# Second MLP: the first products of the last three tiles put ahead of the output products of tiles 13 to 17, with a third lnT buffer and a second l16 buffer

## The chip, the core and the metric

The kernel runs on one core of a Trainium2 chip. The metric is the device time of one execution in microseconds (us); less is better. The core has a matrix engine (TensorE, PE in the profile, its weight loads PEld), three engines for elementwise work (VectorE = DVE, ScalarE = ACT, GpSimd = POOL), and SyncE (SP), whose queue here issues all DMAs. Each engine works through its own instructions in the order in which they were written; semaphores tie the engines together.

## The reference

Three stages follow each other: a linear attention, a first MLP with a leaky ReLU, and a second MLP with a softmax-gated activation, a layer norm and an output product. The change is in the second MLP alone:

```python
def _moe2_ref(x, w_in, w_out, g_ln):          # x 2304 x 512, w_in 512 x 1024, w_out 1024 x 512
    h = x @ w_in                              # "first product"
    e = np.exp(h - np.max(h, axis=-1, keepdims=True))
    sm = e / (np.sum(e, axis=-1, keepdims=True) + 1e-09)
    solu = h * sm
    mu = np.mean(solu, axis=-1, keepdims=True)
    var = np.mean((solu - mu) ** 2, axis=-1, keepdims=True)
    ln = (solu - mu) / np.sqrt(var + 1e-06) * g_ln
    return (ln @ w_out).astype(np.float32)    # "output product"
```

## The kernel before

The 2304 tokens are 18 tiles of 128 tokens, numbered 0 to 17 here. Each float32 operand of a large product is held as two fp16 parts (a value cut to fp16 and the remainder), and a product is three groups of fp16 matmuls: high by high, high by low, low by high.

**The stages of one tile in the second MLP.** In the text, inN is the first product of tile N, outN its output product, lnTN and l16N its buffers.

- **inN** (`mlp2_in`, line L1177): 24 matmuls of 128x512 on PE, three groups of 8, into a PSUM buffer h2 (h in the rows, as the profile leaves buffer numbers out). There are two h2 buffers.
- **The middle** (`mlp2_mid`), mostly on DVE: the row maximum mx (L1203), nb (L1205), on ACT the exponential e with its sum (L1208), then three small steps (L1212 to L1214) and so = h*e*r (L1215), which is the last reader of the h2 buffer. Then the two halves of the statistics (L1220), their aggregate (L1221), ve (L1222), on POOL the power rs (L1223), rs scaled (L1227), the normalised ln (L1228, shown as e because it takes a buffer of that pool), on POOL its fp16 part l16 (L1233), on DVE the remainder (L1235). Two small steps of the following tile, u (L1192, L1194), stand among these.
- **The transposes** (L1240): two DMA transposes issued by SP bring the two halves of l16 into a buffer lnT.
- **outN** (`mlp2_out`, line L1253): 24 matmuls of 128x512 which read lnT as weights, into a PSUM buffer h1 (also two).
- **The store** (`store`): ACT copies h1 with a scale into osb (L1262), one buffer, and SP issues the DMA to the output (L1268, or two DMAs at L1271 for a tile that is split over two sequences, as tile 17 is).

**What sets the order.** The program's order is made when the kernel is built, by the class `Issue`: an event simulation in which every stage is a generator with a priority (a lower number goes first), buffers are counted as room, and each engine takes the ready piece of work with the lowest priority number. A product is queued in pieces of 8 matmuls. What comes out is a fixed list of instructions for each engine; on the chip, an engine whose next instruction has to wait stands still, even if a later one could run. The second MLP's outputs have priority 1002, its first products 1003 up to a tile number z, and those from z on 1001. So a first product with 1003 is put into the list only where no output product is ready, and one with 1001 goes ahead of every output product as soon as an h2 buffer is free.

```python
    BUFS = dict(raw=2, scr=2, hl=2, T=2, ke=4, qe=2, qf=2, qT=2, x=2, x16=2, kv16=2, a=2, h1=2, y=2, xT=2,
                lk=2, g32=2, wraw=3, sg=1, v=2, kv=1, y16=1, h2=2, o=1, e2=2, so=1, l16=1, lnT=2, osb=1, v16=1, kf=2)
    BUFS.update(X["bufs"])
    ...
            if z < NTILE:                                    # at the end of mlp2_in(a, z)
                yield "go", mlp2_in(z, NTILE), 1001
    ...
        sch.go(mlp2_out(), 1002)
        sch.go(mlp2_in(0, NTILE - X["tail"]), 1003)
```

Before, `tail` is 1: only in17 has the priority 1001. There are two lnT buffers and one l16 buffer.

Of the kernel before, what the change touches and what calls it, by code (L numbers as in the profile page):

```python
# [21 lines left out]

X = {'NF': 1, 'EQ': [0, 1], 'bufs': {'qe': 2, 'v': 2, 'qf': 1, 'ke': 2, 'hl': 1, 'x': 4, 'g': 6, 'sg': 3, 'qT': 4, 'x16': 2, 'scr': 3, 'T': 2, 'kf': 2, 'v16': 1, 'wraw': 3, 'raw': 2, 'y16': 1}, 't0': 418.54, 'tb': 82.11, 'w1': 131.17, 'w1s': 10.01, 'w2': 172.22, 'w2s': 4.94, 'b0': -3.87, 'b1': 157.98, 'dk': 3.59, 'dq': 11.23, 'dl': 4.75, 'c1': 81.02, 'c2': 330.62, 'pw2': 700.82, 'wlo': [0, 2, 8, 10, 12, 13, 23, 24, 25, 26, 29, 31, 33, 35, 37, 38, 40, 41, 42, 44, 45, 46], 'vd': 431.89, 'warm': 10, 'psq': ['k11', 'k14', 'k15', 'k2', 'k3', 'k5', 'k7', 'q0', 'q1', 'q12', 'q15', 'q5', 'q8', 'q9'], 'ya': [1, 2, 3, 9, 12, 13, 14, 16, 17, 18, 20, 21, 22, 23, 25, 26, 28], 'EK': [0, 1, 2, 3, 4, 5, 8], 'pkv': 528.48, 'tail': 1, 'sg': [0, 8, 9, 10, 11, 14, 15, 17, 18, 19, 21, 22, 26, 27, 28, 29, 30, 31], 'off': {'w13': -14.7, 'w5': -30.7, 'w14': 26.4, 'k1': -250.2, 'q1': -363.9, 'w2': 350.0, 'w15': -88.3, 'w4': 32.0, 'w10': -33.7, 'w23': 200.4, 'w18': 88.3, 'w24': 240.3, 'w28': -174.0, 'q17': 307.2, 'w1': -201.9, 'q10': 28.7, 'k8': 106.6, 'w21': -43.9, 'k2': 79.3, 'k15': -121.9, 'k3': -134.3, 'w20': -29.3, 'w26': 230.4, 'w6': 31.1, 'q5': 23.9, 'k6': -67.8, 'w7': -53.2, 'q3': -0.6, 'w16': -93.6, 'w25': -25.5, 'w12': 100.4, 'w9': 46.6, 'w19': -77.9, 'w0': 3.9, 'k16': -35.8, 'w17': -13.4, 'k13': 66.1, 'q15': -91.7, 'w31': 51.4, 'k14': 90.6, 'q6': 57.8, 'q7': -18.0, 'w22': 30.7, 'w8': 14.0, 'k11': -16.2, 'q14': -55.4, 'v1': 138.2, 'e2': 31.5, 'w29': 42.1, 'e1': -2.7, 'k5': -29.3, 'q13': -19.5, 'q16': -120.7, 'q11': -76.4, 'e3': 84.3, 'w3': 4.5, 'w30': 16.0, 'v0': -191.6, 'k0': -35.0, 'v3': -23.5, 'k17': 33.4, 'k9': -8.2, 'q12': 2.6, 'k10': 46.2, 'k4': 9.0, 'w27': -9.0, 'q2': 3.1, 'q0': 4.3, 'q9': -1.0, 'v2': -1.6}, 'pe': -759.15, 'KH': [2, 3], 'vb': 544.54}


class Issue:
# [126 lines left out]
def linear_attention_moe_kernel(  # L155
# [29 lines left out]
    KW = 72  # L185
    NG0, NG = NP, X["bufs"].get("g", 7)
    NX = 3
    NF = X["NF"]
    EQ = X["EQ"]
    off = X["off"].get  # L190

# [49 lines left out]

    BUFS.update(X["bufs"])
    sch = Issue(dict(BUFS, g0=NG0, g=NG, v16=0))
# [54 lines left out]
    def cut(x, s, h, l, e="V2"):  # L298

        yield "op", "A", 0.61, lambda: A.activation(out=h, in_=x, func=AF.Copy, scale=s)  # L300
        yield "op", e, 0.67, lambda: V.scalar_tensor_tensor(
            out=l, in0=x, scalar=s, in1=h, op0=ALU.mult, op1=ALU.subtract)

    def cut_weight(n, x, s, h, l):

        if n not in X["wlo"]:
            yield from cut(x, s, h, l)
# [1050 lines left out]
```

## Time and profile before

| what | value |
|---|---|
| time, median of 3 runs | 735.59 us (735.02 to 735.67) |
| the profiled execution's own time | 737.42 us |
| its span (first to last instruction of the profile) | 735.6 us |
| PE busy in the span | 697.9 us, 95% |
| DVE busy | 517.4 us, 70% |
| ACT busy | 385.4 us, 52% |
| POOL busy | 163.3 us, 22% |
| granted PE clock, mean | 0.963 |

The first row is what counts. The profile shows one execution: its span, the busy time of each engine, and for each idle stretch of an engine what ended it. The granted clock is the share of PE's full clock that was allowed: 1.00 is its upper level of 2.4 GHz, 0.50 its lower level of 1.2 GHz; a value between is a mean over both.

### The profile page before, as it was taken

What the parts mean: (1) busy time and instruction counts of PE and PEld (TensorE: products, weight loads), DVE (VectorE), ACT (ScalarE), POOL (GpSimd) and SP (SyncE); (2) the same over time, 40 slices, a digit from 0 to 9 for tenths busy, and PEclk for the clock granted to TensorE, in tenths of its full rate; (3) what the DMA queues carried; (4) which work ended last, traced back from release to release, by engine and by line L of the source; (5) the groups of instructions that cost most, each with busy time, mean ns of one, the idle gap of its engine ahead of it and who ended that gap; (6) DMA issues with size and microseconds to landing.
All of it is one profiled execution on the core that took longest, in us unless ns stands there. A gap on an engine that the chain in (4) does not pass through costs nothing.

```text
span 735.6 us, 13252 instructions
## 1 busy us (share of the span) xinstructions
PE 697.9 (95%) x4888; PEld 451.9 (61%) x4888; DVE 517.4 (70%) x1351; ACT 385.4 (52%) x854; POOL 163.3 (22%) x205
## 2 busy tenths in 40 slices
PE   5967899999999999999999999999999999999977
PEld 3957788656775775767757667566654444444432
DVE  5889898899888656977756428974078577577571
ACT  5797699767787754677725425655132121221120
POOL 3233344522621101112101002353001102011110
PEclk7965899999999999999999999999999999999997
DMA  9588976449757441574315434711024324314232
GB/s 272 165 252 217 229 228 172 93 105 155 143 74 153 105 102 44 103 140 75 59 29 86 73 94 161 211 38 30 1 44 86 94 50 87 85 44 108 65 81 62
DMA packets 183984, 81.21 MB, mean 110 GB/s; under 512 B 146800, under 2 KB 175472, under 8 KB 183920
## 3 DMA queue, kind: packets, MB, share of 16 engines
q1 hardware_dynamic: 183920, 80.38, 47.8%
q8 instruction: 38, 0.62, 0.3%
q14 instruction: 26, 0.21, 0.1%
HBM read 41.75 MB, written 4.72 MB: 63 GB/s over the span
## 4 chain that ended last, share of the span: by engine, by line
PE 80%; DMA 6%; DVE 6%; ACT 3%; issue 2%; SPq 1%; POOL 0%; ACTq 0%; DVEq 0%; POOLq 0%
PE y L1063 20%; PE h L1018 18%; PE h L1253 13%; PE h L1177 13%; PE h L1012 3%; PE y L1059 3%; PE kv L788 2%; DMA T<-hl 2%; DMA qT<-qf 2%; PE a L708 1%; PE a L927 1%; PE a L709 1%; PE kv L783 1%; DMA raw<-in_k_dram 1%; PE a L705 1%
## 5 line engine op out<-in xcount | busy, mean ns | idle before, releaser
L1063 PE MATMUL y<-w,g 128*128 128x512 f16 x768 | 175.4, 379 | 0.3 <-DVE g L1036 0.3
L1018 PEld LDWEIGHTS <-w 128*128 128x128 f16 x1536 | 148.2, 98 | 24.9 <-issue 1.6
L1063 PEld LDWEIGHTS <-g 128*128 128x128 f16 x768 | 73.5, 98 | 78.9 <-DVE g L1036 0.8
L1018 PE MATMUL h<-xy,w 128*128 128x256 f16 x960 | 110.9, 273 | 0.5 <-DVE g L1036 0.4
L1253 PE MATMUL h<-wo,lnT 128*128 128x512 f16 x432 | 98.8, 387 | 4.7 <-DMA lnT<-l 4.7
L1253 PEld LDWEIGHTS <-lnT 128*128 128x128 f16 x432 | 42.9, 100 | 57.9 <-DMA lnT<-l 5.2
L1177 PE MATMUL h<-wi,xy 128*128 128x512 f16 x336 | 75.5, 379 | 0.0
L1034 ACT ACTIVATE h<-h 128x512 f32<-128x512 f32 x64 | 38.1, 595 | 68.5 <-PE h L1018 68.1
L1036 DVE TENSOR_TENSOR g<-h,g 128x512 f16<-128x512 f32 x64 | 43.9, 686 | 37.3 <-ACT g L1035 37.1
L1018 PE MATMUL h<-xT,w 128*128 128x256 f16 x576 | 67.8, 272 | 0.2
L1208 ACT ACTIVATE e<-h,nb,u 128x1024 f32<-128x1024 f32 x18 | 21.7, 1203 | 67.7 <-DVE nb L1205 56.6
L727 ACT ACTIVATE qe<-a,nb,sc 128x128 f32<-128x128 f32 x128 | 47.6, 466 | 17.5 <-DVE nb L718 10.6
L1177 PEld LDWEIGHTS <-xy 128*128 128x128 f16 x336 | 32.9, 98 | 38.8
L715 DVE TENSOR_REDUCE mx<-a 128x4 f32<-128x512 f32 x63 | 42.8, 684 | 16.4 <-PE a L709 12.7
L1262 ACT ACTIVATE osb<-h,c_out 128x512 f32<-128x512 f32 x18 | 12.4, 687 | 78.3 <-PE h L1253 42.0
L894 POOL TENSOR_SCALAR qf<-qe 128x512 f16<-128x512 f32 x32 | 21.6, 675 | 127.2 <-DMA qT<-qf 58.6
L1223 POOL TENSOR_TENSOR rs<-ve,mhalf 128x1 f32<-128x1 f32 x18 | 9.9, 549 | 156.1 <-DVE ve L1222 146.3
L1035 ACT ACTIVATE g<-h 128x512 f16<-128x512 f32 x64 | 38.4, 601 | 1.2
L727 ACT ACTIVATE ke<-a,nb,sc 128x128 f32<-128x128 f32 x88 | 33.0, 487 | 10.4 <-DVE nb L718 9.3
L1203 DVE TENSOR_REDUCE mx<-h 128x1 f32<-128x1024 f32 x18 | 21.9, 1219 | 16.1 <-PE h L1177 16.1
L708 PE MATMUL a<-omA,T 128*128 128x128 f16 x216 | 30.7, 226 | 2.1 <-DMA T<-hl 1.9
L897 DVE SCALAR_TENSOR_TENSOR qf<-qe,qf 128x512 f16<-128x512 f32 x32 | 25.3, 791 | 10.0 <-POOL qf L894 9.9
(190 smaller groups left out, 1215.1 us busy)
## 6 DMA issues: line engine op xcount, KB each, us to landing
wraw<-in_moe_w_in_dram SPq DMA_DIRECT2D x24, 512.0 KB, 5.6
wraw<-in_moe_w_out_dram SPq DMA_DIRECT2D x24, 512.0 KB, 3.3
v<-in_v_dram SPq DMA_DIRECT2D x12, 512.0 KB, 5.2
raw<-in_k_dram SPq DMA_DIRECT2D x8, 512.0 KB, 4.4
raw<-in_q_dram SPq DMA_DIRECT2D x8, 512.0 KB, 4.3
out_dram<-osb SPq DMA_DIRECT2D x16, 256.0 KB, 2.3
v<-in_v_dram SPq DMA_DIRECT2D x6, 128.0 KB, 3.8
lnT<-l SPq DMA_TRANSPOSE x36, 3.2
```

The lines of the kernel that those rows point to most:

```text
L708: PE.matmul(ps[:, h, :], lhsT=st["T"][:, 2 * h + hh, :], rhs=omA, start=True, stop=False)
L715: yield "op", "V", 0.6, lambda: V.tensor_reduce(out=mx, in_=w["ps"], axis=AX.X, op=ALU.max)
L727: A.activation(out=t[:, h, :], in_=w["ps"][:, h, :], func=AF.Exp, scale=st["sc"], bias=w["nb"][:, h:h + 1])
L897: yield "op", "V2", 0.6, lambda: V.scalar_tensor_tensor(out=w["f"][:, :, 1, :], in0=w["e"], scalar=2.0 ** 14, in1=w["f"][:, :, 0, :], op0= ...
L1012: PE.matmul(ps[:, f, :], lhsT=stash(w1, c * KC + kc)[:, o:o + 128], rhs=xT[j][:, kc, :], start=(kc == 0), stop=(kc == KC - 1))
L1018: PE.matmul(ps[:, f, :], lhsT=w1[:, c * KC + kc, w, o:o + 128], rhs=xT[j][:, :, xo + kc, :], start=(n == 0), stop=(n == 3 * KC - 1))
L1034: yield "op", "A", 0.48, lambda: A.activation(out=ps, in_=ps, func=AF.Prelu, scale=2.0 ** -19, alpha=0.01)
L1035: yield "op", "A", 0.48, lambda: A.activation(out=gg[:, 0], in_=ps, func=AF.Copy)
L1036: yield "op", "V", 0.6, lambda: V.tensor_tensor(out=gg[:, 1], in0=ps, in1=gg[:, 0], op=ALU.subtract)
L1063: PE.matmul(y_ps[j][t], lhsT=gg[:, a, f, ts], rhs=w2[:, 2 * p + f, w, :], start=(ends[0] and f == 0 and n == 0), stop=(ends[1] and f == 1 ...
L1177: PE.matmul(ps[:, f, :], lhsT=yT[i][:, a + c, :], rhs=W["i"][:, 2 * c + f, w, :], start=(j == 0 and c == 0), stop=(j == 2 and c == KC - 1))
L1253: PE.matmul(ps, lhsT=t[:, a, f, :], rhs=W["o"][:, f, w, :], start=(j == 0 and f == 0), stop=(j == 2 and f == KF2 - 1))
```

## The change

Three numbers in the table `X` change: `tail` from 1 to 3, so that in15, in16 and in17 have the priority 1001, and two new entries in `bufs`: three lnT buffers in place of two, two l16 buffers in place of one. Both lie in one pool of SBUF. The core of the diff (the line is the whole table; the rest of it is the same):

```diff
-X = {'NF': 1, ... 'raw': 2, 'y16': 1}, 't0': 418.54, ... 'tail': 1, ...
+X = {'NF': 1, ... 'raw': 2, 'y16': 1, 'lnT': 3, 'l16': 2}, 't0': 418.54, ... 'tail': 3, ...
```

Since the order comes out of the build, the built programs tell what moves. In the lists below h2, xy and xT are a first product's target and input, h1 and lnT those of an output product; the numbers behind a name tell one allocation from another.

**PE, the end of its list.** Only the first matmul of each run of equal ones is shown (their weight loads are left out); a run is 24 matmuls, or part of them where the same target comes again. Before, from the last third of in14 (h2_8545) on: out12 (h1_8631), in15 (h2_8643) with out13 (h1_8706) inside, in16 (h2_8753) with out14 (h1_8773) inside, in17 (h2_8845), out15, out16, out17:

```order
L1177 MATMUL h2_8545<-wi_6395,xy7_1975 128x512
...
L1253 MATMUL h1_8631<-wo_6396,lnT_8591 128x512
...
L1177 MATMUL h2_8643<-wi_6395,xy7_1975 128x512
...
L1253 MATMUL h1_8706<-wo_6396,lnT_8664 128x512
...
L1177 MATMUL h2_8753<-wi_6395,xT_6073 128x512
...
L1253 MATMUL h1_8773<-wo_6396,lnT_8731 128x512
...
L1177 MATMUL h2_8845<-wi_6395,xT_6073 128x512
...
L1253 MATMUL h1_8886<-wo_6396,lnT_8856 128x512
...
L1253 MATMUL h1_8953<-wo_6396,lnT_8942 128x512
...
L1253 MATMUL h1_8983<-wo_6396,lnT_8964 128x512
```

With the change, from the same place: out12 (h1_8626) in three pieces of 8 matmuls, with in15 (h2_8651), in16 (h2_8702) and in17 (h2_8767) whole between and behind them, then out13 to out17 in a row:

```order
L1177 MATMUL h2_8545<-wi_6395,xy7_1975 128x512
...
L1253 MATMUL h1_8626<-wo_6396,lnT_8578 128x512
...
L1177 MATMUL h2_8651<-wi_6395,xy7_1975 128x512
...
L1177 MATMUL h2_8702<-wi_6395,xT_6073 128x512
...
L1177 MATMUL h2_8767<-wi_6395,xT_6073 128x512
...
L1253 MATMUL h1_8788<-wo_6396,lnT_8664 128x512
...
L1253 MATMUL h1_8878<-wo_6396,lnT_8757 128x512
...
L1253 MATMUL h1_8920<-wo_6396,lnT_8844 128x512
...
L1253 MATMUL h1_8955<-wo_6396,lnT_8903 128x512
...
L1253 MATMUL h1_8983<-wo_6396,lnT_8944 128x512
```

out13 and out14 have moved behind in17; the number of matmuls is the same. Ahead of this place PE's list is unchanged.

**SP, the end of its queue.** The transposes of a tile (two, of one shape) and the stores of results. Before, from the transposes of tile 12 on:

```order
L1240 DMA_TRANSPOSE lnT_8591<-l16_8577 128x8x128 x2
L1268 DMA out_0_dram<-osb_8628 128x512
L1240 DMA_TRANSPOSE lnT_8664<-l16_8633 128x8x128 x2
L1268 DMA out_0_dram<-osb_8692 128x512
L1240 DMA_TRANSPOSE lnT_8731<-l16_8720 128x8x128 x2
L1268 DMA out_0_dram<-osb_8750 128x512
L1268 DMA out_0_dram<-osb_8820 128x512
L1240 DMA_TRANSPOSE lnT_8856<-l16_8826 128x8x128 x2
L1268 DMA out_0_dram<-osb_8937 128x512
L1240 DMA_TRANSPOSE lnT_8942<-l16_8930 128x8x128 x2
L1240 DMA_TRANSPOSE lnT_8964<-l16_8952 128x8x128 x2
L1268 DMA out_0_dram<-osb_8984 128x512
```

With the change, from the same place (the last store, of tile 17, follows in both):

```order
L1240 DMA_TRANSPOSE lnT_8578<-l16_8564 128x8x128 x2
L1268 DMA out_0_dram<-osb_8627 128x512
L1240 DMA_TRANSPOSE lnT_8664<-l16_8633 128x8x128 x2
L1240 DMA_TRANSPOSE lnT_8757<-l16_8740 128x8x128 x2
L1268 DMA out_0_dram<-osb_8789 128x512
L1240 DMA_TRANSPOSE lnT_8844<-l16_8811 128x8x128 x2
L1268 DMA out_0_dram<-osb_8879 128x512
L1240 DMA_TRANSPOSE lnT_8903<-l16_8874 128x8x128 x2
L1268 DMA out_0_dram<-osb_8921 128x512
L1240 DMA_TRANSPOSE lnT_8944<-l16_8933 128x8x128 x2
L1268 DMA out_0_dram<-osb_8956 128x512
L1268 DMA out_0_dram<-osb_8984 128x512
```

The transposes of tile 14 now stand ahead of the store of tile 12, those of tile 15 between the stores of tiles 12 and 13, those of tile 16 between the stores of 13 and 14 (before, behind the store of 15), those of tile 17 between the stores of 14 and 15.

**DVE, one of three like places** (tiles 3, 8 and 13; here tile 3). A piece of the difference, with its + and -:

```order
 L1203 TENSOR_REDUCE mx2_7675<-h2_7583 128x1
 L1192 TENSOR_SCALAR u_7683<-ikv_tok_94,ix_tok_95,c_h2_97 128x1
+L1235 TENSOR_TENSOR l16_7693<-e2_7671,l16_7693 128x1024
 L1205 TENSOR_SCALAR nb2_7676<-mx2_7675,u_7592 128x1
 L1194 TENSOR_SCALAR u_7683<-u_7683,iy_tok_96 128x1
-L1235 TENSOR_TENSOR l16_7706<-e2_7671,l16_7706 128x1024
 L1212 TENSOR_SCALAR sm_7677<-sm_7677 128x1
```

The remainder of the tile before (L1235) has moved from behind nb, on which this tile's exponential waits, to ahead of it. At the end of DVE's list the middles of tiles 15, 16 and 17 follow each other in the interleaved order that tiles 16 and 17 have before: the maximum of one tile between the statistics of the tile before, the remainder of the tile before behind so.

## Rows read from the trace of the kernel before

**Rows 1.** The page, parts 1 and 2: PE's busy time; granted clock by fortieths.

```profile
PE 697.9 (95%) x4888; PEld 451.9 (61%) x4888; DVE 517.4 (70%) x1351; ACT 385.4 (52%) x854; POOL 163.3 (22%) x205
PEclk7965899999999999999999999999999999999997
```

**Rows 2.** Stretches: length; busy PE, PEld, DVE, ACT, POOL; granted clock; DMA share; GB/s.

```profile
535.00:676.25 141.25, 141.25 (x662) 64.58 (x661) 100.46 (x217) 30.08 (x48) 22.30 (x28) 1.00 0.35 73
712.50:717.20 4.70, 0.02 (x2) 0.01 (x1) 3.96 (x7) 0.69 (x1) 1.17 (x2) 0.87 0.63 145
717.20:723.00 5.80, 5.80 (x15) 2.10 (x16) 2.18 (x3) 0.00 (x0) 1.04 (x1) 0.52 0.48 93
723.00:730.50 7.50, 7.47 (x35) 3.20 (x33) 0.00 (x0) 0.69 (x1) 0.00 (x0) 1.00 0.15 47
```

**Rows 3.** Waits from 535 us to the end: total, times, longest.

```profile
PE h L1253 <- DMA lnT<-l: 4.7, 1, 4.7
POOL l L1233 <- DMA lnT<-l: 4.2, 3, 1.4
```

**Rows 4.** The chain that ended last, from 660 us: start, length, what.

```profile
676.25 5.18 PE h L1253 x24
...
713.82 3.33 DMA lnT<-l
...
717.19 13.29 PE h L1253 x48
```

**Rows 5.** Timeline: the middle of tile 14, and the last products. (Start, length, engine, line.)

```profile
676.29 1.23 DVE L1203 TENSOR_REDUCE mx<-h 128x1 f32<-128x1024 f32 x1 [1.67 <-PE h L1177]
...
680.85 1.28 DVE L1215 SCALAR_TENSOR_TENSOR so<-h,r,e 128x1024 f32<-128x1024 f32 x1
...
681.52 0.69 ACT L1262 ACTIVATE osb<-h,c_out 128x512 f32<-128x512 f32 x1 [1.34 <-issue]
...
682.17 1.29 DVE L1220 BATCH_NORM_STATS2 bn<-so 128x6 f32<-128x512 f32 x2
...
713.31 0.34 SPq L1268 DMA_DIRECT2D out_dram<-osb  x1
...
714.81 1.28 DVE L1220 BATCH_NORM_STATS2 bn<-so 128x6 f32<-128x512 f32 x2
...
718.53 1.04 POOL L1233 TENSOR_SCALAR l<-e 128x1024 f16<-128x1024 f32 x1 [1.38 <-DMA lnT<-l]
719.61 1.23 DVE L1235 TENSOR_TENSOR l<-e,l 128x1024 f16<-128x1024 f32 x1 [1.41 <-POOL l L1233]
```

**Rows 6.** Timeline of two interleaved middles, tiles 11 and 12.

```profile
655.61 0.70 DVE L1220 BATCH_NORM_STATS2 bn<-so 128x6 f32<-128x512 f32 x1
656.23 1.21 DVE L1203 TENSOR_REDUCE mx<-h 128x1 f32<-128x1024 f32 x1
657.35 0.68 DVE L1220 BATCH_NORM_STATS2 bn<-so 128x6 f32<-128x512 f32 x1
657.95 0.20 DVE L1205 TENSOR_SCALAR nb<-mx,u 128x1 f32<-128x1 f32 x1
...
660.29 1.04 POOL L1233 TENSOR_SCALAR l<-e 128x1024 f16<-128x1024 f32 x1 [1.19 <-DVE sm L1212]
...
660.69 1.28 DVE L1215 SCALAR_TENSOR_TENSOR so<-h,r,e 128x1024 f32<-128x1024 f32 x1
...
661.89 1.22 DVE L1235 TENSOR_TENSOR l<-e,l 128x1024 f16<-128x1024 f32 x1
...
663.02 1.28 DVE L1220 BATCH_NORM_STATS2 bn<-so 128x6 f32<-128x512 f32 x2
```

**Rows 7.** Timeline: so of tile 13.

```profile
669.92 1.28 DVE L1215 SCALAR_TENSOR_TENSOR so<-h,r,e 128x1024 f32<-128x1024 f32 x1
```

**Rows 8.** The tile lnT over the span: its transposes, and their landing after issue.

```profile
L1240 SPq DMA_TRANSPOSE lnT<-l x36: 1232/1278/2082, 543.9 to 720.9; - x36
...
DMA to landing us min/median/max: 3.0/3.2/4.3
```

More of the change, by code (lines that the diff above doesn't have):

```diff
@@ L16 @@
 PSUM = bass.MemoryType.PSUM
-X = {'NF': 1, 'EQ': [0, 1], 'bufs': {'qe': 2, 'v': 2, 'qf': 1, 'ke': 2, 'hl': 1, 'x': 4, 'g': 6, 'sg': 3, 'qT': 4, 'x16': 2, 'scr': 3, 'T': 2, 'kf': 2, 'v16': 1, 'wraw': 3, 'raw': 2, 'y16': 1}, 't0': 418.54, 'tb': 82.11, 'w1': 131.17, 'w1s': 10.01, 'w2': 172.22, 'w2s': 4.94, 'b0': -3.87, 'b1': 157.98, 'dk': 3.59, 'dq': 11.23, 'dl': 4.75, 'c1': 81.02, 'c2': 330.62, 'pw2': 700.82, 'wlo': [0, 2, 8, 10, 12, 13, 23, 24, 25, 26, 29, 31, 33, 35, 37, 38, 40, 41, 42, 44, 45, 46], 'vd': 431.89, 'warm': 10, 'psq': ['k11', 'k14', 'k15', 'k2', 'k3', 'k5', 'k7', 'q0', 'q1', 'q12', 'q15', 'q5', 'q8', 'q9'], 'ya': [1, 2, 3, 9, 12, 13, 14, 16, 17, 18, 20, 21, 22, 23, 25, 26, 28], 'EK': [0, 1, 2, 3, 4, 5, 8], 'pkv': 528.48, 'tail': 1, 'sg': [0, 8, 9, 10, 11, 14, 15, 17, 18, 19, 21, 22, 26, 27, 28, 29, 30, 31], 'off': {'w13': -14.7, 'w5': -30.7, 'w14': 26.4, 'k1': -250.2, 'q1': -363.9, 'w2': 350.0, 'w15': -88.3, 'w4': 32.0, 'w10': -33.7, 'w23': 200.4, 'w18': 88.3, 'w24': 240.3, 'w28': -174.0, 'q17': 307.2, 'w1': -201.9, 'q10': 28.7, 'k8': 106.6, 'w21': -43.9, 'k2': 79.3, 'k15': -121.9, 'k3': -134.3, 'w20': -29.3, 'w26': 230.4, 'w6': 31.1, 'q5': 23.9, 'k6': -67.8, 'w7': -53.2, 'q3': -0.6, 'w16': -93.6, 'w25': -25.5, 'w12': 100.4, 'w9': 46.6, 'w19': -77.9, 'w0': 3.9, 'k16': -35.8, 'w17': -13.4, 'k13': 66.1, 'q15': -91.7, 'w31': 51.4, 'k14': 90.6, 'q6': 57.8, 'q7': -18.0, 'w22': 30.7, 'w8': 14.0, 'k11': -16.2, 'q14': -55.4, 'v1': 138.2, 'e2': 31.5, 'w29': 42.1, 'e1': -2.7, 'k5': -29.3, 'q13': -19.5, 'q16': -120.7, 'q11': -76.4, 'e3': 84.3, 'w3': 4.5, 'w30': 16.0, 'v0': -191.6, 'k0': -35.0, 'v3': -23.5, 'k17': 33.4, 'k9': -8.2, 'q12': 2.6, 'k10': 46.2, 'k4': 9.0, 'w27': -9.0, 'q2': 3.1, 'q0': 4.3, 'q9': -1.0, 'v2': -1.6}, 'pe': -759.15, 'KH': [2, 3], 'vb': 544.54}
@@ new lines @@
+X = {'NF': 1, 'EQ': [0, 1], 'bufs': {'qe': 2, 'v': 2, 'qf': 1, 'ke': 2, 'hl': 1, 'x': 4, 'g': 6, 'sg': 3, 'qT': 4, 'x16': 2, 'scr': 3, 'T': 2, 'kf': 2, 'v16': 1, 'wraw': 3, 'raw': 2, 'y16': 1, 'lnT': 3, 'l16': 2}, 't0': 418.54, 'tb': 82.11, 'w1': 131.17, 'w1s': 10.01, 'w2': 172.22, 'w2s': 4.94, 'b0': -3.87, 'b1': 157.98, 'dk': 3.59, 'dq': 11.23, 'dl': 4.75, 'c1': 81.02, 'c2': 330.62, 'pw2': 700.82, 'wlo': [0, 2, 8, 10, 12, 13, 23, 24, 25, 26, 29, 31, 33, 35, 37, 38, 40, 41, 42, 44, 45, 46], 'vd': 431.89, 'warm': 10, 'psq': ['k11', 'k14', 'k15', 'k2', 'k3', 'k5', 'k7', 'q0', 'q1', 'q12', 'q15', 'q5', 'q8', 'q9'], 'ya': [1, 2, 3, 9, 12, 13, 14, 16, 17, 18, 20, 21, 22, 23, 25, 26, 28], 'EK': [0, 1, 2, 3, 4, 5, 8], 'pkv': 528.48, 'tail': 3, 'sg': [0, 8, 9, 10, 11, 14, 15, 17, 18, 19, 21, 22, 26, 27, 28, 29, 30, 31], 'off': {'w13': -14.7, 'w5': -30.7, 'w14': 26.4, 'k1': -250.2, 'q1': -363.9, 'w2': 350.0, 'w15': -88.3, 'w4': 32.0, 'w10': -33.7, 'w23': 200.4, 'w18': 88.3, 'w24': 240.3, 'w28': -174.0, 'q17': 307.2, 'w1': -201.9, 'q10': 28.7, 'k8': 106.6, 'w21': -43.9, 'k2': 79.3, 'k15': -121.9, 'k3': -134.3, 'w20': -29.3, 'w26': 230.4, 'w6': 31.1, 'q5': 23.9, 'k6': -67.8, 'w7': -53.2, 'q3': -0.6, 'w16': -93.6, 'w25': -25.5, 'w12': 100.4, 'w9': 46.6, 'w19': -77.9, 'w0': 3.9, 'k16': -35.8, 'w17': -13.4, 'k13': 66.1, 'q15': -91.7, 'w31': 51.4, 'k14': 90.6, 'q6': 57.8, 'q7': -18.0, 'w22': 30.7, 'w8': 14.0, 'k11': -16.2, 'q14': -55.4, 'v1': 138.2, 'e2': 31.5, 'w29': 42.1, 'e1': -2.7, 'k5': -29.3, 'q13': -19.5, 'q16': -120.7, 'q11': -76.4, 'e3': 84.3, 'w3': 4.5, 'w30': 16.0, 'v0': -191.6, 'k0': -35.0, 'v3': -23.5, 'k17': 33.4, 'k9': -8.2, 'q12': 2.6, 'k10': 46.2, 'k4': 9.0, 'w27': -9.0, 'q2': 3.1, 'q0': 4.3, 'q9': -1.0, 'v2': -1.6}, 'pe': -759.15, 'KH': [2, 3], 'vb': 544.54}
```

## The prediction, as put on record before the changed kernel ran

> **What bounds the kernel now.** I began with the page. PE is busy for 697.9 of 735.6 us, and its granted clock is at 9 tenths or more in every fortieth but the first few and the last [rows 1]. So the kernel ends when PE is through its list, and what can be gained lies at the two ends of the span. The change touches the second MLP, so I cut its time into stretches. From 535 to 676.25 us PE is busy for 141.25 of 141.25 us at a clock of 1.00; from 712.50 to 717.20 it does nothing; from 717.20 to 723.00 it works at a clock of 0.52, and from 723.00 to its end at 1.00 again [rows 2]. The waits name the one that ends last: from 535 us on PE waits once, for 4.7 us, for the DMA that fills lnT; POOL waits three times for a free l16, 4.2 us in all, while PE stands still for none of these three [rows 3]. The chain of work shows the same: out12 from 676.25, at the end the transpose of tile 16 landing (3.33 us from 713.82), then out16 and out17, 13.29 us for 48 matmuls [rows 4].
>
> The price of one matmul comes from the chain: 5.18 us for the 24 of out12, 0.2158 each [rows 4]. From 676.25 PE still has out12 to out17 and in15 to in17, nine products or 216 matmuls, 46.62 us of work. It ends at 717.19 + 13.29 = 730.48, after 54.23 us [rows 4]. So **7.61 us** are lost there: 4.7 idle [rows 3], and 2.9 because the 48 matmuls at the end take 13.29 us in place of 48 x 0.2158 = 10.36 [rows 4], the half clock of [rows 2].
>
> Why it waits: tile 16's chain through DVE, POOL and the transposes is the last but one, and behind in17 PE has only out15 to do, 5.18 us. The first transpose of tile 16 was issued at 713.82, behind the store of tile 15 in SP's queue (713.31) [rows 4, 5].
>
> **The change, step by step.** No instruction is added or taken away, so the work stays at 46.62 us from 676.25. The question is whether each product finds its input. I lay PE's new list out without waits and hold every chain against it. A third of a product is 1.73 us. out12 first third 676.25 to 677.98; in15 to 683.16; second third to 684.89; in16 to 690.07; last third to 691.80; in17 to 696.98; out13 to 702.16; out14 to 707.34; out15 to 712.52; out16 to 717.70; out17 to 722.88.
>
> *The h2 buffers.* in16 takes the one of tile 14, which is free when so of tile 14 is done: 680.85 + 1.28 = 682.13 [rows 5], 2.8 us before in16 starts at 684.89. in17 takes that of tile 15. Its middle starts with the maximum: in15 ends at 683.16, the statistics of tile 14 keep DVE until 683.46 [rows 5], so it starts there. In the interleaved middles so starts 4.46 us behind the maximum (656.23 to 660.69) [rows 6]; here the second statistics half does not lie between (0.60, from 657.35 to 657.95 [rows 6]), which leaves 3.86. So of tile 15: 687.3 to 688.6, 3.2 us ahead of in17 at 691.80.
>
> *The chain of tile 16.* From so to the remainder is 1.20 and to the statistics 2.33 (660.69, 661.89, 663.02), and 0.62 later the next maximum starts (655.61, 656.23) [rows 6]. So the maximum of tile 16 starts at 687.3 + 2.95 = 690.25 (in16 ends at 690.07), its so at 694.7, the maximum of tile 17 at 697.7, so of tile 17 at 702.1, and the remainder of tile 16 at 703.3 to 704.5. ACT's copy of out12 stands in its list ahead of tile 16's exponential and can hold that up by its 0.69 [rows 5]; I leave it out, since the margins below are larger. SP has the store of tile 13 ahead of tile 16's transposes: out13 ends at 702.16, ACT starts 0.09 later (out12 ended at 676.25 + 5.18 = 681.43, its copy began at 681.52) and takes 0.69, the store's issue 0.34 [rows 4, 5], so 703.3. The first transpose is issued then, the second 1.28 later at 704.6, and each lands 3.2 us after its issue, 4.3 at the most [rows 8]: 707.8 (708.9) against out16's start at 712.52. **Margin 4.7 us.**
>
> *The chain of tile 17.* Statistics at 704.5; from there to l16 on POOL takes 3.7 (714.81 to 718.53) and to the remainder 4.8 (719.61), 1.23 long [rows 5]: 709.3 to 710.5. SP's store of tile 14 is out by 708.5. The transposes are issued at 709.3 and 710.6 and land at 713.8 (714.9), against 717.70. **Margin 3.9 us.** lnT13 and lnT14, whose buffers tiles 16 and 17 take over, are free at 702.16 and 707.34, both ahead of the issues.
>
> *The buffers.* That out13 to out17 can wait in a row needs room for several finished tiles: tile 15's transposes take lnT12 (free at 691.80), while lnT13 and lnT14 stay full. The second l16 buffer takes POOL's three waits of 4.2 us away [rows 3]; PE waits for none of them, so I set it at 0. Bounds: below 0 lies nothing but a little margin, above 0 nothing that PE could give back ahead of 712.50, where it has no idle time [rows 2].
>
> *The remainder moved ahead of nb* (three places) delays that tile's exponential by at most its 1.22 us [rows 6]. The last is tile 13, whose so ended at 669.92 + 1.28 = 671.20 [rows 7]; in15 takes its h2 buffer at 677.98. With 5.6 us to spare I set it at 0; without that cover it would be 1.22 for each place, 3.7 in all.
>
> *Behind PE.* From the last matmul to the end of the span 735.6 - 730.48 = 5.12 us pass for copy and stores [rows 4]; the same instructions stand there after.
>
> **The sum.** Both losses go: 735.6 - 7.61 = 728.0 for the span. The profiled execution's own time, 737.42, is 1.8 above its span, and the median of the runs shown, 735.59, lies at the span, so I carry the difference over to the median: 735.59 - 7.61 = **728.0 us**, 1.0% less.
>
> On the half clock: the granted clock was 1.00 up to 712.50, the engine then stood still for 4.7 us, and the clock read 0.52 in the stretch behind and 1.00 after that [rows 2]. In the second MLP it is low only behind this pause, so I let the 2.9 us go with the pause. If the clock fell for some other reason at that place, they stay, and the time is 735.59 - 4.7 = 730.9. The Trainium skill, "TensorE: Matmul & The Clock Gate", part 1, says that an engine that pauses falls to half rate and gets the full rate back by sustained work; this trace agrees. By that rule, too, the time is 728.0, not 730.9.
>
> **The rivals.** *Part of the wait stays (B).* In the tail three middles lie close together, one per 6.91 us of PE (in plus a third), while an interleaved one takes 7.4 of DVE (655.61 to 663.02 [rows 6]). If DVE or POOL hold each other up more than in the rows, out16 or out17 waits again. POOL's l16 keeps its 1.04 us beside a busy DVE and alike when DVE waits for it [rows 5, 6], which speaks against it. If 2 us more were lost for each of three middles, 6 in all, the margin of 3.9 would be overrun by 2.1: 728.0 + 2.1 = 730.1, and with the half clock again 733.0.
> The Trainium skill, "SBUF — State Buffer", section "SBUF: two separate sides", says that DVE and GpSimd share a port pair as an exclusive lock, so that the second comer waits out the whole instruction of the first. No pair of rows above shows such a wait; by that rule a busier DVE would lead to rival B.
>
> *Nothing comes of it (C).* The wait moves to another place of like size, for example in front of in16 (margin 2.8), with the half clock behind it: about 735.6. Its margin speaks against it. PE's list shows that the products do move, so that the change does nothing is excluded.
>
> *Slower (D).* PE works strictly in order, so with in17 ahead of out13 to out17 a late so of tile 15 stops five products whose inputs are ready; before, they would have run. A wait w there costs w, and if it is about as long as the present one, 2.9 more for the clock. The kernel is as before at w = 4.7 and slower by 0.2% (1.5 us) at w = 6.2, that is, if so of tile 15 ended at 698.0 in place of 688.6. At w = 8 the time is 738.9. The middles of before speak against it: from the maximum to the end of so is 5.7 us in the rows [rows 6], and D needs 14.5.
>
> **How the numbers follow.** 728.0 with both losses gone: 0.76. B: 0.13. C: 0.04. D: 0.04. The rest, 0.03, is a larger gain than I can name. A measurement of this kernel can tell about 0.2%, 1.5 us, from no change. Faster takes the forecast, nearly all of B and the rest, 0.91; same 0.04; slower 0.05, D and the worst of B. The range reaches up to 731.0, which takes in the sum with the half clock left (730.9) and the milder half of B, and down to 727.0, for the 0.2 to 0.3 us that each chain reading is uncertain by, on several of them.
>
> **What would show it.** Right: PE without an idle stretch from 535 us to its last matmul, granted clock 1.00 to the end, the last matmul near 722.9, the transposes of tiles 16 and 17 landed some 4 us before out16 and out17 begin, no wait of PE for lnT. The steps are wrong if PE waits in front of in16 or in17 (then so was late), if out16 or out17 waits (B), or if the clock reads below 1.00 in the last 20 us without a pause before it.

## The result and the profile after

The changed kernel takes 728.73 us (median of 4 runs, 727.12 to 729.64) against 735.39 us of the kernel before on the same chip; the ratio is 0.9907, with a 95% interval of 0.9887 to 0.9928. That is 6.8 us less (5.3 to 8.3). 728.0 had been forecast.

The stretches of the changed kernel, in the columns of [rows 2]; the second runs from the start of out12 to behind the last matmul:

```profile
535.00:676.25 141.25, 141.25 (x663) 64.64 (x661) 100.50 (x217) 30.10 (x48) 21.58 (x28) 1.00 0.34 73
676.25:723.00 46.75, 46.67 (x217) 20.93 (x214) 28.79 (x59) 8.51 (x13) 7.15 (x9) 1.00 0.38 90
```

PE is busy all the way at a granted clock of 1.00: the idle stretch of 4.70 us and the one at 0.52 of [rows 2] have no counterpart. The chain that ended last, in its last pieces, goes through PE alone:

```profile
676.30 1.73 PE h L1253 x8
678.03 5.18 PE h L1177 x24
683.21 1.73 PE h L1253 x8
684.94 5.18 PE h L1177 x24
690.12 1.73 PE h L1253 x8
691.85 5.18 PE h L1177 x24
697.02 25.91 PE h L1253 x120
```

These are out12 in thirds with in15, in16 and in17, then out13 to out17 as one run of 120 matmuls to 722.93; in [rows 4] the chain leaves PE for a transpose. The page's group of output products shows it too (busy, mean ns of one, idle before):

```profile
L1253 PE MATMUL h<-wo,lnT 128*128 128x512 f16 x432 | 95.9, 379 | 0.0
```

For comparisons I use one length, the **tail**: from the first matmul of out12 to the end of the last matmul, by PE's timeline. Before it is 54.37 us (676.09 to 730.46), by these first and last rows:

```profile
676.09 5.34 PE L1253 MATMUL h<-wo,lnT 128*128 128x512 f16 x24
...
717.19 13.27 PE L1253 MATMUL h<-wo,lnT 128*128 128x512 f16 x48 [4.68 <-DMA lnT<-l]
```

After, it is 46.78 us (676.14 to 722.92), 7.59 less:

```profile
676.14 1.89 PE L1253 MATMUL h<-wo,lnT 128*128 128x512 f16 x8
...
696.86 26.06 PE L1253 MATMUL h<-wo,lnT 128*128 128x512 f16 x120
```

In these rows the last matmul of a run counts with its own 0.379 us, one that another follows at once with 0.2158. So a pause costs 0.16 us more than the idle time that the row shows, and 24 matmuls at full pace read 5.34, 48 read 10.52. The 7.59 us are 4.68 + 0.16 for the pause and 2.75 (13.27 - 10.52) for the slow stretch behind it.

### The profile page after: what moved, and what is told of

Same layout as the page of the kernel before. It is cut to its first block, busy times and chain, and to the rows that moved or that the text cites. A ratio compares the mean times of both kernels' runs of the same rounds, so it can differ in the third digit from the quotient of the medians.

```text
span 727.8 us, 13253 instructions
## 1 busy us (share of the span) xinstructions
PE 693.6 (95%) x4888; PEld 450.7 (62%) x4888; DVE 513.2 (71%) x1351; ACT 386.0 (53%) x854; POOL 164.4 (23%) x205
## 4 chain that ended last, share of the span: by engine, by line
PE 80%; DMA 7%; DVE 6%; ACT 3%; issue 2%; SPq 1%; POOL 0%; DVEq 0%; ACTq 0%
PE y L1063 20%; PE h L1018 16%; PE h L1253 13%; PE h L1177 13%; PE h L1012 4%; PE y L1059 3%; PE kv L788 2%; PE a L708 2%; DMA T<-hl 2%; PE a L709 2%; PE a L927 2%; DMA wraw<-in_moe_w_in_dram 1%; DMA qT<-qf 1%; PE kv L783 1%; PE a L705 1%
## 5 line engine op out<-in xcount | busy, mean ns | idle before, releaser
L1253 PE MATMUL h<-wo,lnT 128*128 128x512 f16 x432 | 95.9, 379 | 0.0
L1012 PE MATMUL h<-xT,w 128*128 128x256 f32 x128 | 31.5, 399 | 0.8 <-DVE ar L326 0.8
```

The costliest lines, as they stand in the source:

```text
L1012: PE.matmul(ps[:, f, :], lhsT=stash(w1, c * KC + kc)[:, o:o + 128], rhs=xT[j][:, kc, :], start=(kc == 0), stop=(kc == KC - 1))
L1253: PE.matmul(ps, lhsT=t[:, a, f, :], rhs=W["o"][:, f, w, :], start=(j == 0 and f == 0), stop=(j == 2 and f == KF2 - 1))
```

## The experiments

The theory: PE's own order is the whole gain. PE waited because too little of its work stood between in16 or in17 and the products that need their results; the pause costs its length and, behind it, a stretch at half clock. The rivals: the buffers are what pays; the half clock has another cause; three tiles ahead are not needed, or more are better.

**1. The buffers alone.** The changed kernel with its buffers, but

```diff
-'tail': 3
+'tail': 1
```

> The changed kernel's three lnT and two l16 buffers, with tail left at 1. Theory (the order alone removes PE's wait): the end is as before, PE idle for about 4.7 us ahead of out16 and out16 at the half clock; time 735 to 736, within 0.2% of before. Rival (the buffers are what pays, since POOL waited 4.2 us for l16 and tiles 15 to 17 need room for finished results): the transposes of tile 16 come earlier and at least 3 us are gained, 732 or less.

Measured: 734.81 us, ratio 0.9993 (0.9979 to 1.0007), the same. The waits from 535 us on have PE's pause still in, and POOL's wait for l16 (4.2 us in [rows 3]) is gone:

```profile
PE h L1253 <- DMA lnT<-l: 4.6, 1, 4.6
```

The buffers alone give nothing that can be told. The tail is 53.17 us (676.33 to 729.50), 1.20 shorter than before, and nearly all of that lies behind the pause: out16 and out17 took 12.12 us here against 13.27 before. The granted clock (columns of [rows 2]) came back earlier here; before, it was 0.52 in the mean up to 723 us:

```profile
717.38 12.12 PE L1253 MATMUL h<-wo,lnT 128*128 128x512 f16 x48 [4.63 <-DMA lnT<-l]
717.40:720.00 2.60, 2.60 (x7) 0.95 (x8) 1.31 (x3) 0.00 (x0) 1.04 (x1) 0.50 0.21 39
720.00:723.00 3.00, 3.00 (x14) 1.30 (x13) 0.88 (x1) 0.00 (x0) 0.00 (x0) 0.89 0.73 141
```

So the same list of PE with a pause of like length paid 1.60 us for the half clock here and 2.75 in the profiled execution of before.

**2. The order alone.** Tail 3 in the kernel before, its two lnT and one l16 buffers kept:

```diff
-'tail': 1
+'tail': 3
```

> Tail 3 with the old buffers, two lnT and one l16. Theory (the order alone): worked out from the trace of the changed kernel, the transposes of tiles 16 and 17 are held back by the buffers, first transpose of tile 16 issued at about 708.5 and landed at 711.6, 0.9 us ahead of out16; of tile 17 issued at 714.0 and landed at 717.1, 0.6 us ahead of out17. So PE still does not wait, and the time is that of the changed kernel, 727 to 729. Rival (without the buffers the new order only moves the wait): out16 or out17 waits 2 us or more, time 731 or more.

Measured: 728.28 us, ratio 0.9902 (0.9882 to 0.9922), as the changed kernel. The tail is 47.09 us, 0.31 longer. Of its waits from 535 us on these two tell the story:

```profile
POOL l L1233 <- DMA lnT<-l: 16.4, 6, 4.9
...
PEld L1253 <- DMA lnT<-l: 0.6, 1, 0.6
```

POOL waits 16.4 us for the one l16 buffer, which the transposes hold until lnT is free, and PE pays 0.31 us for it. So in the change the buffers are a reserve and the order is the gain. The reserve was thinner than worked out: a margin of 0.6 us ahead of out17 was expected, and out17 started 0.31 us late, so the working was off by 0.9.

**3. Two tiles ahead in place of three.** The changed kernel with

```diff
-'tail': 3
+'tail': 2
```

> The changed kernel with tail 2 in place of 3: in16 and in17 ahead, in15 where it was. Theory (what counts is how much PE work lies between in17 and out17, against the about 11.5 us from the maximum of tile 17 to its first transpose and 3.1 for landing): in17 would end at 703.9, the first transpose lands at 717.7 to 718.6, out17 is reached at 717.7, so PE waits 0 to 1 us; time 728 to 729.5. Rival (three tiles ahead are needed): half of the gain or less, 731.5 or more.

Measured: 729.71 us, ratio 0.9924 (0.9904 to 0.9944). The tail is 48.65 us, 1.87 longer than with three; PE waits twice, and both products behind the waits run at full pace (5.35):

```profile
702.03 8.80 PE L1253 MATMUL h<-wo,lnT 128*128 128x512 f16 x40
711.27 5.35 PE L1253 MATMUL h<-wo,lnT 128*128 128x512 f16 x24 [0.44 <-DMA lnT<-l]
717.71 5.35 PE L1253 MATMUL h<-wo,lnT 128*128 128x512 f16 x24 [1.08 <-DMA lnT<-l]
```

Two tiles give most of the gain (the rival had expected half or less). I had out17's wait right at up to 1 us and had not seen out16's 0.44. The time does not tell two from three, the intervals overlap; the tails of the two profiled executions do, by two waits that can be seen.

**4. Tail 4, with four lnT buffers.**

```diff
-'lnT': 3, 'l16': 2} ... 'tail': 3
+'lnT': 4, 'l16': 2} ... 'tail': 4
```

> Tail 4 with four lnT and two l16 buffers: in14 too ahead of the outputs, which are then out13 to out17 at the end with out12's like cut into the first products. Theory (the gain is the end of PE's wait, and there is none left): PE's stretch from out12's place on stays at 46.7 us, time 727 to 730, ratio as for the changed kernel. Rival (more distance gives more): a further gain of 1 us or more.

Measured: 729.01 us, ratio 0.9920 (0.9898 to 0.9942). From 660 us to its end at 721.74 PE has no wait, as with three. More distance gives nothing, because nothing is left to hide.

**5. The pause filled.** The kernel before, with matmuls on constant weights in PE's pause; their target is overwritten by out16, so they add work and change no result:

```diff
             ps = mk(ps_1, "h1", [128, DM], F32)
             t = lnT.pop(i)
+            if i == 16:
+                for _ in range(22):
+                    PE.matmul(ps, lhsT=W["o"][:, 0, 0, 0:128], rhs=W["o"][:, 0, 0, :], start=True, stop=True)
```

> The kernel before, with 22 extra matmuls of 128x512 on constant weights put ahead of out16, 4.7 us of work, about as long as PE's pause; their result is overwritten. Theory (the half clock behind the pause belongs to the pause): out16 and out17 run at the full clock and 2.9 us are gained, 732.5 to 733.0, while the pause itself is still paid. Rival (the clock falls there for another reason, so that of the change's gain only 4.7 us could come from the pause): the stretch behind still reads about 0.5, time 735.4 or more.

Measured: 733.99 us, ratio 0.9981 (0.9963 to 0.9998), which is 1.4 us less than before (0.1 to 2.7) where 2.9 was expected. PE's timeline has the extra matmuls, then out16 and out17 at full pace:

```profile
712.64 4.91 PE L1252 MATMUL h<-wo 128*128 128x512 f16 x22
717.43 5.35 PE L1256 MATMUL h<-wo,lnT 128*128 128x512 f16 x24
723.09 5.35 PE L1256 MATMUL h<-wo,lnT 128*128 128x512 f16 x24 [0.30 <-DMA lnT<-l]
```

The theory holds in kind: the same place, with PE kept at work, runs at the full clock (out16 in 5.35 us), so the half clock belongs to the pause. In size it gave back 2.31 us of the tail (52.06) and not 2.9: the slow stretch had cost 2.75, and out17 now waits for its own transposes (0.30 + 0.16), a wait that the slow out16 had covered.

**6. The pause filled, with the new buffers.** The same edit on the kernel of experiment 1.

> The kernel before with the 22 extra matmuls in PE's pause and, besides, the changed kernel's buffers (tail 1). In the run with the extra matmuls alone out17 came to wait 0.3 us for its transposes, which had been hidden behind the half clock, and POOL had waited 1.4 us for l16. Theory: with a second l16 buffer that wait shrinks to 0 to 0.3 us, PE's last matmul ends 51.8 to 52.1 us after the start of out12 (52.06 with the extra matmuls alone, 54.37 before), time 0.2 to 0.4% below before. Rival (the half clock comes back at this place whatever PE did before): out16 runs 1.5 us or more longer than 5.35.

Measured: 733.43 us, ratio 0.9973 (0.9953 to 0.9993). The tail is 51.95 us, and out17's wait is down to 0.15:

```profile
712.05 5.35 PE L1256 MATMUL h<-wo,lnT 128*128 128x512 f16 x24
717.56 5.35 PE L1256 MATMUL h<-wo,lnT 128*128 128x512 f16 x24 [0.15 <-DMA lnT<-l]
```

Experiment 1 is its control, with the same buffers and the pause left empty: the filling takes 1.22 us off the tail (53.17 - 51.95), the 1.60 of that slow stretch less out17's new wait (0.15 + 0.16), to within 0.1. Here too the clock goes with the pause; its price differs between the two pairs because the slow stretch itself did.

**7. The margin of the last tile.** The changed kernel, with extra statistics instructions into a scratch tile in the middle of tile 17, 10 in one kernel and 16 in the other:

```diff
+        def aggr():
+            if i == 17:
+                bx = tiny.tile([128, 6], F32, name="bx", tag="bx", bufs=1)
+                for _ in range(10):
+                    V.bn_stats(out=bx, in_=so[:, 0:512])
+            V.bn_aggr(out=mv, in_=bn)
-        yield small(lambda: V.bn_aggr(out=mv, in_=bn))
+        yield small(aggr)
```

> The changed kernel with 10 extra statistics instructions of 128x512 on DVE (0.645 us apart, 6.5 us in all) in the middle of tile 17, ahead of the aggregate of its statistics, so that its l16 and transposes come 6.5 us later. By the step of the prediction that counted both transposes against the start of out17 (margin 3.9 us) PE waits 2.6 us and the time is 730.5 or more. By the landing of the first transpose alone, which the trace of the changed kernel has 5.7 us ahead of out17, it waits 0.8 us; time about 728.8.

Measured: 729.86 us, ratio 0.9932 (0.9904 to 0.9960). PE's last rows and the transposes:

```profile
694.08 20.88 PE L1259 MATMUL h<-wo,lnT 128*128 128x512 f16 x96
713.20 2.60 SPq L1246 DMA_TRANSPOSE lnT<-l  x2
716.47 5.35 PE L1259 MATMUL h<-wo,lnT 128*128 128x512 f16 x24 [1.51 <-DMA lnT<-l]
```

In the changed kernel tile 17's first transpose is issued 12.10 us behind the start of out13 (696.86 to 708.96), here 19.12: the delay came out as 7.02. PE is idle for 1.51 of it and starts out17 1.67 later (with the 0.16), so the margin is 5.35 us. The landing of the first transpose had given 5.7, the step of the prediction 3.9.

> The same with 16 extra statistics instructions, 10.3 us. By the margin of 3.9 us PE waits 6.4 us, by that of 5.7 us 4.6 us, each with up to 2.9 us more where the clock falls behind it: 735 to 738, or 732.5 to 736. A longer wait than 4.7 us ahead of the one last product would also show whether only pauses of some length bring the half clock.

Measured: 736.35 us, ratio 1.0015 (0.9999 to 1.0031):

```profile
694.41 20.88 PE L1259 MATMUL h<-wo,lnT 128*128 128x512 f16 x96
717.90 2.60 SPq L1246 DMA_TRANSPOSE lnT<-l  x2
721.13 6.83 PE L1259 MATMUL h<-wo,lnT 128*128 128x512 f16 x24 [5.84 <-DMA lnT<-l]
```

A delay of 11.39 (717.90 - 694.41 = 23.49, less 12.10), a wait of 5.84 + 0.16: a margin of 5.39, as good as the same. This time the half clock follows, out17 takes 6.83 us in place of 5.34. The tail is 54.27 us, nearly that of before (54.37), by the last tile alone.

**8. Rival D made on purpose.** The changed kernel, with 10 extra statistics instructions ahead of so of tile 15, the last reader of the h2 buffer that in17 takes:

```diff
+        def add():
+            if i == 15:
+                bx = tiny.tile([128, 6], F32, name="bx", tag="bx", bufs=1)
+                for _ in range(10):
+                    V.bn_stats(out=bx, in_=e[:, 0:512])
+            V.tensor_scalar(out=sm, in0=sm, scalar1=1e-9, scalar2=None, op0=ALU.add)
-        yield small(lambda: V.tensor_scalar(out=sm, in0=sm, scalar1=1e-9, scalar2=None, op0=ALU.add))
+        yield small(add)
```

> The changed kernel with 10 extra statistics instructions on DVE, 6.5 us, in the middle of tile 15 ahead of so, the last reader of its h2 buffer. Rival D's mechanism, made on purpose: so of tile 15 ends at about 694.9 in place of 688.4, in17 waits 3.1 us for the h2 buffer (margin 3.2), and PE, working in order, stands still though out13 and out14 are ready; time 728.7 + 3.1 = 731.8, and up to 2.9 more if the clock falls. If PE could pass in17 by, or the margin were larger, less than 1 us is lost.

Measured: 733.79 us, ratio 0.9991 (0.9973 to 1.0010); the tail is 52.27 us:

```profile
688.29 1.89 PE L1259 MATMUL h<-wo,lnT 128*128 128x512 f16 x8
693.99 6.87 PE L1177 MATMUL h<-wi,xT 128*128 128x512 f16 x24 [3.81 <-DVE so L1221]
700.69 26.06 PE L1259 MATMUL h<-wo,lnT 128*128 128x512 f16 x120
```

PE stands still for 3.81 us in front of in17, with out13 ready behind it, and in17 itself takes 6.87 in place of 5.34. Together with the 0.16 that is 5.5 us, most of the gain. The mechanism of rival D is real; what keeps it away is its margin.

**9. The last store from two queues.** The changed kernel, with the second of tile 17's two stores on ACT's queue:

```diff
-                    SP.dma_start(out=out[c * S + S4:(c + 1) * S, :], in_=o[p:p + n])
+                    (A if i == 17 and p else SP).dma_start(out=out[c * S + S4:(c + 1) * S, :], in_=o[p:p + n])
```

> The changed kernel, with the second of the two stores of tile 17 issued by ACT in place of SP, so that both are issued at once behind the last copy. The two issues took 1.12 us on SP one behind the other, so by the trace about 0.5 us of the 4.9 us behind PE's last matmul goes: a span about 0.5 us shorter from the last matmul on, not visible in the time (0.07%). If the stores share a bound elsewhere, nothing changes.

Measured: 727.08 us, ratio 0.9900 (0.9868 to 0.9933), not to be told from the changed kernel. Both stores are issued at once:

```profile
722.25 0.69 ACT L1262 ACTIVATE osb<-h,c_out 128x512 f32<-128x512 f32 x1 [4.49 <-PE h L1253]
722.96 0.49 SPq L1271 DMA_DIRECT2D out_dram<-osb  x1
722.96 0.55 ACTq L1271 DMA_DIRECT2D out_dram<-osb  x1
```

From the last matmul (722.16) to the end of the span (726.7) pass 4.54 us against 4.88 in the changed kernel (722.92 to 727.8), some 0.3 less where 0.5 was expected. It costs nothing, and the time cannot show it.

## Why the prediction was right

**What bounds the tail** was read rightly: PE's list, with one wait in it. With the list without waits PE's end was worked out as 722.88, and it came at 722.92. What was foreseen is the length, 46.62 us of work and 0.16 for the end of the last matmul, against 46.78. That the point in time fits as well is luck: out12 started at 676.14 here and at 676.09 before, but between 670.96 and 676.38 in the profiles of the experiments.

**The steps on the h2 buffers and the chains** came out close. These are the rows of DVE, POOL and SP in the changed kernel, of so of tile 15, the maximum, so and remainder of tile 16, so of tile 17, and the transposes of tiles 16 and 17:

```profile
687.15 1.29 DVE L1215 SCALAR_TENSOR_TENSOR so<-h,r,e 128x1024 f32<-128x1024 f32 x1
...
690.16 1.22 DVE L1203 TENSOR_REDUCE mx<-h 128x1 f32<-128x1024 f32 x1
...
694.63 1.28 DVE L1215 SCALAR_TENSOR_TENSOR so<-h,r,e 128x1024 f32<-128x1024 f32 x1
...
702.02 1.28 DVE L1215 SCALAR_TENSOR_TENSOR so<-h,r,e 128x1024 f32<-128x1024 f32 x1
...
703.22 1.22 DVE L1235 TENSOR_TENSOR l<-e,l 128x1024 f16<-128x1024 f32 x1
703.46 2.64 SPq L1240 DMA_TRANSPOSE lnT<-l  x2
...
708.96 2.60 SPq L1240 DMA_TRANSPOSE lnT<-l  x2
```

Forecast were 687.3, 690.25, 694.7, 702.1, 703.3, 703.3 and 709.3. An order that the kernel before already ran on two tiles [rows 6] gave the spacing for three. The remainder moved ahead of nb, set at 0, costs nothing that PE shows: ahead of out12 it is busy for 141.25 of 141.25 us after as before. That move came with the buffers (DVE's list has it in experiment 1, not in experiment 2).

**The margin of the last tile** was too small by 1.5 us: 3.9 in the prediction, 5.35 and 5.39 measured in experiment 7. I had both transposes landed before the product starts. But the first 16 matmuls of a product read only the first half of lnT, and the chain of before showed it already, where out16 started at 717.19 with the first transpose landed at 713.82 + 3.33 [rows 4]. Besides, the first transpose was issued 0.34 us earlier than forecast; the rows that gave its time held l16 up by the old buffer [rows 5]. Both made the forecast more cautious and did not change the sum.

**The buffers at 0** is shown by experiments 1 and 2 in both directions. What I wrote of them, that out13 to out17 can wait in a row only with room for several finished tiles, is wrong: with the old buffers tile 15's transposes wait for lnT13 and still come in time.

**The half clock** goes with the pause, as said; experiments 5 and 6 show it at the very place. Its size was read from one execution: 2.9 us, of which about 0.16 is the last matmul's own length, so 2.75. In experiment 1 a pause of like length cost 1.60 (12.12 against 10.52 for 48 matmuls at full pace). The profiled tails differ by 7.59 us and the times by 6.8 (5.3 to 8.3), so the two agree within the interval. The prediction carried the loss of one execution over to the median; whether the half clock was dearer in that execution than in most is open, since only one execution of each kernel has a trace.

**The rivals.** B did not come about; DVE and POOL held each other up no more than in the rows, as the chain of tile 17 shows: in the tail l16 took 1.04 to 1.05 us on POOL and so 1.28 to 1.29 on DVE, also where the two overlap (l16 of tile 15 from 694.24, so of tile 16 from 694.63). The lock that the prediction takes from the Trainium skill, "SBUF — State Buffer", section "SBUF: two separate sides", is stated there only for DVE instructions in a 2-port mode or, against a GpSimd instruction that reads SBUF, with two SBUF inputs; no wait of that kind shows in these rows. C is excluded by the result. D's margin of 3.2 us was worked out rightly: in experiment 8 so of tile 15 came 7.15 us later behind its maximum (10.88 against 3.73), and in17 started 3.97 late (3.81 + 0.16). Its clock term was not: the half clock cost 1.53 us there, not 2.9.

## What to carry to other kernels

When an engine that works strictly in order is full but for one wait at the end, count its own work between the last producer and the last consumer, and hold that against the chain through the other engines: here about 15 us from the end of in17 to its first landed transpose against the 20.7 us of four outputs; before, the 15.0 us of tile 16 (702.15 to 717.15) had in17 and out15 against them, 10.4 us, and the difference is the pause. The work to put there is work that was ready anyway, which costs nothing to move; buffers belong to the change only if the chain then waits for one, and a long wait of an engine beside the path (16.4 us of POOL in experiment 2) does not say so. A pause of the matrix engine can be paid a second time by the half clock behind it, as those of 3.81 us and more were here and those of up to 1.51 us were not. A step that takes such a pause away gains more than its length; one that only takes the half clock away gains less than the slow stretch cost, where that stretch covered another wait.

## What the runs showed of the hardware that I had not expected

**Which pauses bring the half clock.** Single pauses of 0.44, 1.08 and 1.51 us (experiments 3 and 7) left the next product at 5.35 us. Pauses of 3.81, 4.63, 4.68 and 5.84 us made the work behind them longer by 1.53, 1.60, 2.75 and 1.49 us. In these four the cost does not grow with the pause. What it follows is how long PE works at the low clock. Rows of experiment 8 (the first two) and of the second kernel of experiment 7, in the columns of [rows 2]:

```profile
694.00:696.00 2.00, 2.00 (x5) 0.71 (x6) 2.00 (x3) 0.00 (x0) 0.00 (x0) 0.50 0.00 0
696.00:698.00 2.00, 2.00 (x8) 0.83 (x7) 2.00 (x7) 0.40 (x1) 0.08 (x1) 0.73 0.92 222
715.30:721.10 5.80, 0.00 (x0) 0.00 (x0) 2.19 (x3) 0.00 (x0) 1.39 (x2) 0.68 0.35 67
721.13:724.00 2.87, 2.87 (x7) 1.04 (x8) 0.00 (x0) 0.69 (x1) 0.00 (x0) 0.50 0.48 136
724.00:726.00 2.00, 2.00 (x10) 0.92 (x9) 0.00 (x0) 0.00 (x0) 0.00 (x0) 0.96 0.34 131
```

The length of each working stretch times what its clock lacks to 1.00 gives 1.54 us for experiment 8 (2.00 x 0.50 + 2.00 x 0.27), 1.63 for experiment 1 (2.60 x 0.50 + 3.00 x 0.11), 2.78 for before (5.80 x 0.48) and 1.52 for experiment 7 (2.87 x 0.50 + 2.00 x 0.04), each within 0.03 of the time measured. In experiment 7 the clock was low during part of the pause already (0.68), where it costs nothing, and only the rest fell on work.

**The start of the tail wanders.** The program ahead of out12 is almost the same in all these kernels, yet out12 started at 670.96 us in one profile (experiment 6) and at 676.38 in another (experiment 5). That is as much as most effects studied here, and why I compared tails and not spans. It goes with the execution, not with the kernel alone: the one profiled in experiment 6 took 729.66 us, the fastest of ten of that kernel, with a median of 733.43. The difference is there before 430 us already, since the last product of the attention, which closes at that time, starts 5 us apart in the profiles of before and of experiment 6:

```profile
L927 PE MATMUL a<-kv,qT x432: 190/193/218, 122.8 to 427.7; 128*128 128x65 f16 x112, 128*64 128x65 f16 x32
```

and in experiment 6:

```profile
L927 PE MATMUL a<-kv,qT x432: 190/193/218, 121.0 to 422.7; 128*128 128x65 f16 x112, 128*64 128x65 f16 x32
```

What sets it was not looked into.
